# Window attention and a squared-ReLU layer pair on one core: batch 1 turned by DMA, batch 2 by seven products, 64-row sinks, an order table

## The chip, the core and the metric

The kernel runs on one core of one Trainium2 chip. The metric is device time in microseconds (us). A core has TensorE (PE, matmuls into PSUM), VectorE (DVE), ScalarE (ACT), GpSimd (POOL) and SyncE (SP), each with its own queue of instructions that it runs in program order, and 16 DMA engines. POOL's DMAs here are the ones that convert float32 to bfloat16 on the way (one queue, called q0 in the profile); SP's are plain DMAs and DMA transposes (q1).

## The reference

```python
# q, k, v: (4 batches, 8 heads, 768 positions, 64); n_sink 4, window 128
scores = (1/8) * q @ k^T
keep   = (key < 4) or (0 <= query - key < 128)
a      = softmax(where(keep, scores, -1e9))
x      = (a @ v), heads side by side          # (3072 rows, 512)
out    = max(x @ w_in, 0)**2 @ w_out          # w_in (512, 2048), w_out (2048, 512), float32 out
```

## The kernel before, in words

A batch has 768 rows, worked as three pairs of 128-row tiles (s, or u, = 0, 1, 2). Its stages:

- **Loads.** Batch 0's q and k for the first four tiles come by eight SP DMAs (L557) as float32 and are regrouped to bfloat16. Everything else comes through POOL: tiles of q, k or v (L578, L587, L606, L616; 256 KB read, 128 KB written) and four parts each of w_in (L514) and w_out (L522; 1 MB read, 512 KB written).
- **Turning q and k** so that head dimension lies on partitions. Batches 0 and 1: PE transposes (L708), then copies from PSUM by DVE or ACT. Batches 2 and 3 (`NATURAL`): one DMA transpose per tile on SP (L662), 12 per batch.
- **Attention** per pair of tiles and pair of head pairs (m): scores on PE with 64 rows of the array for each head (L815), exp on ACT (L836), masks on DVE or POOL, values on PE (L884), normalisation on DVE (L900, L901). The four sink keys of all heads are scored by L774 into `es`; for s of 1 and 2 each head's values take one more 128-row matmul `es` x `vs` in which all rows but that head's four are zero.
- **Turning the attention output** (bridge): PE transposes (L933) and copies in batches 0 and 1, DMA transposes on SP (L915) in batches 2 and 3.
- **Layer 1.** Classic (L965): four matmuls per block of 128 hidden units, ReLU on ACT or DVE, square on DVE or ACT. Fast (batch 3, `FAST`): seven products of half size instead of eight (L1085), in six quads; each quad needs sums of x (L1043), a copy and two subtractions of PSUM (L1126), a ReLU, and a final add with ReLU on DVE (L1153). Five sums of w_in (L1009) come first.
- **Layer 2.** Classic (L1174) for the first two pairs of batch 0, else seven products of half size (L1284) with sums of the squares (L1242) and of the results on DVE, then a store by SP.

Every step is an `op` with what it follows, the buffers that it takes and gives back, and the engines that may run it. `Plan.run` writes the program: it always picks the ready step with the earliest start by its own table of costs, changed by `SHIFTS`, a list of offsets for every step. POOL's loads are chained in one fixed order: v tiles 0 and 1, w_in 0, v tiles 2 and 3, the other w_in parts, batch 0's last k and q tiles and v tiles, w_out, then batch 1, 2 and 3.

A product of the fast layer 1 and its following wait, as an example of how steps are tied:

```python
m4 = product(4, 1, 3, False, [k2])      # k2: DVE has taken bank 1 out of PSUM
m3 = product(3, 0, 4, False, [k3])
k4 = op(..., relu, after=[m3, m4], takes=[r1s])
```

Of the kernel before, what the change touches and what calls it, by code (L numbers as in the profile page):

```python
# [12 lines left out]
FP32 = mybir.dt.float32  # L13
BF16 = mybir.dt.bfloat16
# [3 lines left out]
LATENCY = 0.135  # L18
PE_SLACK = 0.0
DMA_START = {"sp": 1.45, "act": 1.2, "pool": 1.6}  # L20
DMA_LATENCY = 0.9
WARM_UNTIL = 34.0
SHIFTS = {
# [9 lines left out]
    ('prep', 0, 0): ((-0.212, 1.23), (-0.072, -0.24), (-0.19, 0.16), (-0.726, 0.34), (0.102, 1.1), (-0.535, 0.02),  # L33
# [3 lines left out]
    ('sink', 0, 0): ((4.752, 1.43), (1.667, 2.03),),  # L37
    ('att', 0, 0): ((0.347, 0.31), (0.954, 0.9), (-0.499, -1.83), (0.762, -2.15), (0.932, -0.05), (-2.305, -7.94),
        (-0.09, 0.64), (-0.608, -0.19),),
    ('val', 0, 0): ((-0.669, 0.31), (-0.697, -0.27), (2.439, -2.91), (-0.554, 0.35), (-0.437, -0.15), (-0.471, 0.35),  # L40
        (-0.386, 0.35), (-0.377, 0.25),),
    ('turn', 0, 0): ((1.726, 0.79), (1.562, 0.69), (1.948, 1.13), (1.496, 0.73),),
    ('att', 0, 1): ((3.244, 0.46), (11.783, 1.08), (3.403, 0.48), (2.622, -0.1), (0.081, -0.49), (-0.044, -0.15),
        (11.287, 1.58), (1.317, -0.32), (2.357, -0.58), (1.537, 1.18), (-0.135, 0.19), (-0.111, -0.81),),
    ('val', 0, 1): ((-1.139, 2.3), (-0.295, 1.56), (-0.887, 1.68), (-0.625, 1.18), (-3.257, -5.22), (-3.374, -3.06),
        (-3.291, -3.92), (-2.551, -2.62),),
    ('turn', 0, 1): ((0.396, -1.51), (-0.815, -0.63), (-0.017, -0.23), (-0.694, 0.15), (-0.252, 1.39),),
    ('prep', 0, 1): ((0.244, -0.3), (0.839, 0.68), (-0.246, 0.32), (0.932, -0.62), (1.027, -0.56), (0.209, -0.32),),
    ('sink', 0, 1): ((1.975, -1.87), (0.782, -1.52),),
    ('att', 0, 2): ((0.244, -0.66), (-1.989, 0.29), (-0.493, 0.33), (0.159, -0.68), (1.032, 0.54), (0.796, 0.57),  # L50
        (-0.189, 0.02), (1.388, -0.12), (0.48, -0.01), (0.313, -0.14), (1.032, 0.72), (-1.933, -0.09),),
    ('val', 0, 2): ((-0.074, -1.39), (-0.782, 0.91), (-0.843, -3.97), (-0.333, 0.47),),
    ('turn', 0, 2): ((0.672, -0.31), (-0.118, -0.09), (0.809, -0.71), (2.596, 0.84),),
# [6 lines left out]
    ('prep', 1, 0): ((-3.284, 0.24), (-1.096, -0.94), (0.605, -0.58), (0.247, -2.12), (-5.483, 0.49), (0.694, 0.02),  # L60
        (0.597, -0.24), (0.597, -0.24), (-8.208, 1.17), (0.681, -1.4), (-1.5, -0.64), (0.357, -0.54), (-10.29, 0.97),
        (0.494, -0.72), (0.633, -0.24), (-0.776, -0.16), (0.529, -0.04), (-1.768, -0.84),),
    ('sink', 1, 0): ((0.868, 0.19), (0.763, 0.03),),
    ('att', 1, 0): ((-0.287, -0.2), (-4.964, -0.65), (-1.435, -0.81), (-3.607, -0.91), (-2.001, -0.01),
        (-0.447, -0.1), (-0.674, 0.1), (-0.719, -0.6), (-0.604, 0.18), (-0.781, -0.2),),
    ('val', 1, 0): ((-6.954, 1.31), (0.072, -4.26), (-0.107, -0.44), (-0.058, -0.46),),
    ('turn', 1, 0): ((-4.522, 0.82), (-0.734, 2.5), (-1.073, 0.44), (0.276, 0.05),),
    ('att', 1, 1): ((1.003, 0.22), (1.223, 0.6), (0.413, -0.45), (0.232, -0.07), (0.259, -0.21), (0.322, -0.07),
        (1.914, -1.56), (0.055, 0.01), (0.085, -2.03), (0.176, 0.47),),
    ('val', 1, 1): ((0.205, 0.29), (-0.249, -0.53), (-2.761, 0.71), (0.377, -0.27),),  # L70
    ('turn', 1, 1): ((0.754, 1.22), (2.068, -0.78), (0.857, 1.68), (-4.788, 1.81),),
    ('prep', 1, 1): ((2.397, 1.96), (5.859, 1.94), (-0.449, 1.75), (1.83, 1.58), (1.97, 1.7), (0.173, -0.21),),
    ('sink', 1, 1): ((0.987, -0.02), (-0.036, -5.62),),
    ('att', 1, 2): ((1.119, -4.28), (0.959, -0.36), (0.499, 1.02), (0.438, -0.34), (1.738, -0.38), (0.767, 0.25),
        (1.547, -0.3), (1.332, 0.31), (1.014, 0.54), (0.269, -2.08),),
    ('val', 1, 2): ((1.128, -0.41), (3.047, 0.37), (3.469, 0.88), (2.416, -3.47),),
    ('turn', 1, 2): ((-4.356, -7.65), (-0.607, -0.19), (-1.006, 0.46), (-4.587, -4.53),),
# [5 lines left out]
    ('sum', 0, 2): ((0.045, -1.68), (0.204, -1.02), (-0.718, -2.55), (0.064, -1.38),),  # L83
# [115 lines left out]
        (0.268, 1.28),),  # L199
    ('ev', 3, 2): ((1.463, 6.42), (-1.377, 1.64), (0.142, -5.03), (-0.286, -3.32), (-0.494, 0.4), (-0.624, -0.94),  # L200
        (-0.804, -0.94), (-1.227, -0.94), (-0.047, -3.46),),
}


class Slot:
# [16 lines left out]
class Plan:  # L222

# [1252 lines left out]
```

## Time and profile before

| | us |
|---|---|
| three runs | 216.72, 217.82, 218.05 (median 217.82) |
| span of the profiled execution | 216.0 |
| PE busy | 206.5 (96%) |
| DVE busy | 161.5 (75%) |
| ACT busy | 123.2 (57%) |
| POOL busy | 98.7 (46%) |
| read from HBM, written | 27.30 MB, 6.29 MB |

The span runs from the first to the last instruction of one execution; the runs are whole executions, so the median is compared with the span through their difference, 1.8 us. A busy PE counts the modelled length of each matmul, which overlaps with the next one's start; how fast matmuls really follow each other is read from the starts. The granted TensorE clock is 1.000. The table of stretches gives, for each stretch, busy us of PE, PE's weight loads, DVE, ACT, POOL with the number of instructions, then granted clock, DMA share and GB/s. In DMA views a queue's share counts the time of its packets, which overlap, so it can be over 100%; its megabytes are those written.

### The profile page before, as it was taken

To read this page: it belongs to the slowest core of one execution; us is meant where nothing else is said; L and a number is where in the kernel's file an instruction comes from. 1 tells how busy PE (TensorE), PEld (TensorE's weight loads), DVE (VectorE), ACT (ScalarE), POOL (GpSimd) and SP (SyncE) were. 2 spreads that over 40 slices of the span, in tenths; PEclk is the share of its full clock that TensorE was granted. 3 is DMA by queue.
4 is the path that set the end of the run, shared out by engine and by line. 5 is a ranking of instruction groups with operands and counts; after the bars stand their busy time and mean duration, and the time that the engine had idled before them with its cause. 6 is when DMAs were issued, how large, how long until landed. Compare 5 with 4: busy or idle time off the path is not lost.

```text
span 216.0 us, 5470 instructions
## 1 busy us (share of the span) xinstructions
PE 206.5 (96%) x2287; PEld 165.4 (77%) x2287; DVE 161.5 (75%) x292; ACT 123.2 (57%) x158; POOL 98.7 (46%) x137
## 2 busy tenths in 40 slices
PE   3999999999999999999999999999999998999993
PEld 3858996689486755688887965598898998897882
DVE  6487458773958569688689994477995859999973
ACT  2498567366663775976757268566623369482100
POOL 7799773698935974898954424002302000000000
PEclk9999999999999999999999999999999999999999
DMA  5999999999997699999999936000023260000133
GB/s 156 261 182 206 174 199 213 160 154 205 156 147 169 88 147 133 167 108 147 142 199 133 139 84 209 3 0 0 3 97 75 52 219 3 2 0 5 55 132 107
DMA packets 93625, 26.09 MB, mean 121 GB/s; under 512 B 86816, under 2 KB 91552, under 8 KB 93600
## 3 DMA queue, kind: packets, MB, share of 16 engines
q0 software_dynamic: 69248, 12.59, 80.3%
q1 hardware_dynamic: 24168, 13.07, 28.1%
q8 instruction: 18, 0.29, 0.6%
q10 hardware_dynamic: 184, 0.07, 0.1%
q14 instruction: 7, 0.06, 0.1%
HBM read 27.30 MB, written 6.29 MB: 156 GB/s over the span
## 4 chain that ended last, share of the span: by engine, by line
PE 73%; DVE 14%; ACT 3%; DMA 3%; issue 3%; SPq 2%; DVEq 0%; ACTq 0%
PE pm L965 29%; PE py L1284 20%; PE po L884 6%; PE py L1174 6%; PE ps L815 5%; PE pm L1085 4%; DMA qr<-in_q_dram 3%; DVE sg L1242 3%; ACT expm L836 2%; DVE t L1126 2%; DVE r L1153 2%; SPq L557 2%; PE px L933 1%; DVE gT_sb L1109 1%; DVE expm L848 1%
## 5 line engine op out<-in xcount | busy, mean ns | idle before, releaser
L965 PE MATMUL pm<-xT,w_in_sb 128*128 128x256 bf16 (+1 forms) x448 | 66.1, 304 | 0.0
L965 PEld LDWEIGHTS <-w_in_sb 128*128 128x128 bf16 x448 | 48.3, 114 | 13.4 <-issue 1.3
L836 ACT ACTIVATE expm<-ps 128x1024 bf16<-128x1024 f32 (+1 forms) x48 | 43.7, 951 | 18.1 <-PE ps L815 17.5
L426 POOL TENSOR_SCALAR_AFFINE_SELECT expm<-expm 128x512 bf16<-128x512 bf16 x36 | 27.3, 787 | 55.9 <-ACT expm L836 43.7
L976 ACT ACTIVATE r<-pm 128x1024 bf16<-128x1024 f32 x30 | 30.7, 1023 | 17.3 <-PE pm L965 15.6
L1284 PEld LDWEIGHTS <-gT_sb 128*128 128x128 bf16 x336 | 31.2, 98 | 4.3 <-issue 0.7
L987 DVE TENSOR_TENSOR gT_sb<-r 128x1024 bf16<-128x1024 bf16 x26 | 19.3, 741 | 17.3 <-ACT r L976 17.1
L1284 PEld LDWEIGHTS <-sg 128*128 128x128 bf16 x240 | 22.4, 98 | 4.5 <-DVE sg L1242 1.0
L1284 PE MATMUL py<-wt,sg 128*128 128x256 bf16 x160 | 20.8, 273 | 0.4 <-DVE sg L1242 0.4
L1284 PE MATMUL py<-wt,gT_sb 128*128 128x256 bf16 x160 | 20.8, 273 | 0.0
L1284 PE MATMUL py<-w_out_sb,gT_sb 128*128 128x256 bf16 x144 | 18.5, 273 | 0.0
L884 PEld LDWEIGHTS <-expm 128*128 128x128 bf16 x352 | 16.3, 97 | 2.5 <-issue 0.7
L901 DVE TENSOR_TENSOR xn_sb<-po,rc 128x512 bf16<-128x512 f32 (+1 forms) x28 | 17.2, 615 | 1.0
L884 PE MATMUL po<-v,expm 128*128 128x65 bf16 x352 | 17.5, 193 | 0.3 <-DVE xT L402 0.2
L1174 PE MATMUL py<-w_out_sb,gT_sb 128*128 128x512 bf16 x64 | 15.3, 380 | 0.0
L848 DVE TENSOR_TENSOR expm<-expm,tri 128x1024 bf16<-128x1024 bf16 x14 | 11.0, 791 | 5.1 <-ACT expm L836 4.9
L815 PE MATMUL ps<-qkT 64*128 64x256 bf16 (+1 forms) x256 | 14.6, 238 | 0.0
L815 PEld LDWEIGHTS <-qkT 64*128 64x128 bf16 x256 | 8.1, 94 | 7.1 <-issue 6.1
L884 PE MATMUL po<-vs,es 128*128 128x65 bf16 x128 | 12.9, 193 | 0.0
L400 ACT ACTIVATE osb<-py 128x256 f32<-128x256 f32 (+1 forms) x15 | 6.6, 441 | 10.2 <-PE py L1284 7.1
L884 PEld LDWEIGHTS <-es 128*128 128x128 bf16 x128 | 11.7, 97 | 0.0
L587 POOL DMA_DIRECT2D v<-in_v_dram x12 | 11.0, 927 | 0.2
(97 smaller groups left out, 330.5 us busy)
## 6 DMA issues: line engine op xcount, KB each, us to landing
out_dram<-osb SPq DMA_DIRECT2D x11, 512.0 KB, 3.7
v<-in_v_dram POOLq DMA_DIRECT2D x24, 128.0 KB, 7.5
qn<-in_k_dram POOLq DMA_DIRECT2D x20, 128.0 KB, 7.5
qn<-in_q_dram POOLq DMA_DIRECT2D x20, 128.0 KB, 7.4
w_in_sb<-in_moe_w_in_dram POOLq DMA_DIRECT2D x4, 512.0 KB, 10.3
w_out_sb<-in_moe_w_out_dram POOLq DMA_DIRECT2D x4, 512.0 KB, 10.2
qr<-in_k_dram SPq DMA_DIRECT2D x4, 256.0 KB, 5.7
qr<-in_q_dram SPq DMA_DIRECT2D x4, 256.0 KB, 5.3
```

Source lines behind the costliest of these rows:

```text
L426: nc.gpsimd.affine_select(out=e_tile, in_=e_tile, compare_op=ALU.is_ge, fill=fill, base=i - 1, pattern=[[0, n], [1 if i else -1, 128]], ch ...
L587: return [nc.gpsimd.dma_start(out=v_sb[b % 2][:, t, :, 0:D], in_=v[b, :, 128 * t:128 * t + 128, :].rearrange("h p d -> p h d"))]
L815: nc.tensor.matmul(ps[:, h2, o:o + w], lhsT=qkT_sb[r, m, 1, c, :], rhs=qkT_sb[r, m, 0, qb:qb + w // 128, :], start=(i == 0 and not biased) ...
L836: nc.scalar.activation(out=x[:, :, o:512], in_=bank_t["s", b, s, m][:, :, o:512], func=AF.Exp, scale=scale)
L848: nc.vector.tensor_mul(y, y, tri.rearrange("p (o a) c -> p o (a c)", o=1).to_broadcast([128, 4, 256]))
L884: touch(("po", b, s, m0), e, nc.tensor.matmul(pv[:, i, h2, :], lhsT=lhsT, rhs=rhs, start=(n_ == 0), stop=(n_ == len(mms) - 1)), j)
L901: touch(("po", b, s, m0), e, nc.vector.tensor_tensor(out=xn_sb[:, 2 * s:2 * s + 2, 128 * (m0 + j0):128 * (m0 + j0 + nj)].rearrange("p i (j ...
L965: nc.tensor.matmul(pm[:, i, :], lhsT=w_in_sb[:, fb // 4, kb, fb % 4:512:4], rhs=xT[:, c0 // 256:(c0 + cw) // 256, kb, :], start=(kb == 0), ...
L976: nc.scalar.activation(out=o, in_=h, func=AF.Relu)
L987: nc.vector.tensor_mul(g, r, r)
L1174: touch((b, u), e, nc.tensor.matmul(pm[:, i, :], lhsT=gT_sb[:, fb, 128 * t:128 * t + 128], rhs=w_out_sb[:, fb, :], start=(fb == 0), stop=( ...
L1284: ins = nc.tensor.matmul(y_, lhsT=x[:, i, :], rhs=r_, start=(first or tail and n == 2) and i == 0, stop=i == HB - 1, skip_group_check=not ...
```

## The change

Six things change together.

1. `NATURAL` becomes (1, 2, 3): batch 1's 12 q and k tiles and its six tiles of attention output are turned by DMA transposes on SP.
2. `FAST` becomes (2, 3): batch 2's layer 1 goes by seven products as well. The sums of w_in are made before batch 2; two of the five overwrite parts of w_in that are no longer read.
3. Sinks: a step of its own ahead of the values, two matmuls of 64 rows and 130 columns for each of two heads' pairs, each on its half of the array and into its own PSUM bank. For that, head pairs m and m + 2 go together where m and m + 1 did.
4. Buffers: PSUM is one pool of four double banks (was two of two), and the work tiles of `expm`, `r` and `sg` share 15 buffers; which buffer a step gets is fixed when the program is written.
5. POOL's loads are no longer chained among themselves.
6. `Plan.run` no longer chooses. The order of all 880 steps, each with its engine (p PE, v DVE, a ACT, g POOL, s SP) and a number of idle-filling matmuls (+n), stands in a table, `ORDER`.

```diff
+ORDER = """
+8s 55a 9s 10s 11s 12s 13s 0v 14s 1v 56v 15s 36g 27g 61v 7a 28g 32g 3g 57p 58p+4 59a 60v 63p+22 33g 31g 67a 6g 19g 5g
+65v 68v 83p 62a 64p+1 69p 73v 75p+8 71v 70p 20g 66a 85a 114p 91p 74a 29g 76p 30g 21g 22g 79g 4g 23g 77v 72v 116a 78v
+104p 93a 107a 92p+1 84p 80v 117v 24g 39g 86a 51g 115p 87p 89p+4 118a 94a 88v 90v 130p 133p+2 37g 135a 81p+1 95p 134v
...
+156p 158p 35g 46g 173a 159v 176a 163p 203s 178p 157a 193p 194a 179a 190p 169p 187p 191a 188a 168v 184p 181p 164v
+170a 165v 180v 185a 174a 47g 268p 189a 219p 43g 34g 264v 182v 269p 222a 186a 345g 44g 200s 363s 347g 352g 201s 54g
+270p 212p 353g 202s 41g 48g 205s 368s 369s 215a 213a 220a 271p 272p 49g 204s 228p 231a 273p 236p 229a 274p 171v 208v
+192v 209v 195v 265v 351g 367s 275p 42g 129g 221v 290v 214v 348g 361g 354g 239a 232v 266v 223v 366s 346g 364s 370s
+177v 237a 254p 279p 276v 280p 277v 360g 374s 358g 357g 586g 359g 372s 238g 588g 255a 257a 216v 246p 210p 371s 278s
...
+234p 242p 235v 350g 183a 296a 283p 284p 243v 245s 365s 226s 258g 250g 285p 300v 244s 293v 259p 260p 261v 298p 301p
+267v 395p 303v 287v 396a 286p 288a 227s 398a 302p 592g 305p 304v 306v 307v 248g 600g 595g 599g 613s 308s 604s 606s
+18s 356g 349g 362g 611s 593g 601g 386p 251p 252p 387a 389a 253v 421p 424a 330p 594g 422a 608s 397v 375v 388v 403p
+315p 598g 596g 589g 406a 407g 404a 390v 331v 391p 377p 316a 378a 262s 263s 587g 399v 405v 392v 318p 379p 319a 380a
+312p 382a 413p 416a 313v 314a 414a 317v 489v 383v 321p 408p 309p 355g 310a 322a 332a 417v 488v 490v 324p 591g 605s
+409p 327p 336p 325a 328a 311v 326v 320a 381v 384p 337a 410v 385v 425v 329a 323a 607s 338a 333p 289s 609s 615s 393s
...
 class Plan:
-    def run(self):
...
+    def run(self, order):
+        for word in order.split():
+            n, _, dummies = word.partition("+")
+            o, e = self.ops[int(n[:-1])], {"p": "pe", "v": "dve", "a": "act", "g": "pool", "s": "sp"}[n[-1]]
...
             o.run(e)
...
-    sizes = dict(att=2, den=2, qr=5, qs=6, expm=8, r=3, osb=2, sg=4, u=2)
+    sizes = dict(ps=4, qr=5, qs=6, w2=15, osb=2, u=2)
...
-    NATURAL, TURNED, BIASED, FAST = (2, 3), (), 1, (3,)
+    NATURAL, TURNED, BIASED, FAST = (1, 2, 3), (), 1, (2, 3)
+    CHAINED = False
...
+                    if s:
+                        def sinks(e, s=s, m0=m0, bo=bo):
+                            po = bank_t["o", b, s, m0] = tile_of(bo, "po", [128, 2, 512], FP32)
+                            for i in range(2):
+                                for j in range(2):
+                                    r, m, c = slice(64 * j, 64 * j + 64), m0 + 2 * j, 128 * (2 * s + i - 2)
+                                    touch(("po", b, s, m0), e, nc.tensor.matmul(
+                                        po[:, j, 2 * (D + 1) * i:2 * (D + 1) * (i + 1)].rearrange("p (h d) -> p h d", h=2),
+                                        lhsT=es[r, c:c + 128], rhs=vs[r, 2 * m:2 * m + 2, :],
+                                        start=(i == 0), stop=False), j)
...
-                                        if t >= 2:
-                                            mms.append((i, h2, es[:, 128 * (t - 2):128 * (t - 2) + 128], vs[:, h, :]))
...
-                nc.vector.tensor_tensor(out=wi_sb[name], in0=x, in1=y, op=how)
+                if n >= 3:
+                    wi_sb[name] = [x[:, 0], x[:, 1]]
+                    nc.vector.tensor_tensor(out=x, in0=x, in1=y, op=how)
+                    return
```

The steps of the table that the prediction speaks of. On POOL: 36g and 33g load w_out parts 3 and 0, 34g part 1; 27g and 28g batch 0's k tiles 4 and 5, 29g and 30g its q tiles 4 and 5; 32g, 31g, 19g, 20g its v tiles 5, 4, 0, 1; 21g loads w_in part 0; 37g to 54g are batch 1's 18 tiles, 345g to 362g batch 2's, 586g to 603g batch 3's (355g is v tile 2 of batch 2). On SP: 196s to 207s turn batch 1's tiles (204s the k tile 4), 226s, 227s, 244s, 245s, 262s, 263s its output, 278s and 308s are stores. On PE: 87p is the first values step of batch 0, 160p its first layer 1 step, 254p the first scores of batch 1's third pair, 409p the first values of batch 2's second pair; 120p, 144p, 109p, 153p, 241p, 233p and so on are sink steps.

More of the change, by code (lines that the diff above doesn't have):

```diff
@@ L299, in run @@
+    def run(self, order):
+        free = {p: list(range(n)) for p, n in self.capacity.items()}
+        emitted = set()
+        for word in order.split():
+            n, _, dummies = word.partition("+")
+            o, e = self.ops[int(n[:-1])], {"p": "pe", "v": "dve", "a": "act", "g": "pool", "s": "sp"}[n[-1]]
+            assert e in o.engines and all(id(a) in emitted for a in o.after + o.follow)
             for s in o.takes:
-                free[s.pool].sort()
-                free[s.pool].pop(0)
@@ L302, in run @@
-            self.now, self.gap = start, start - engine.get(e, 0.0)
+                s.buf = free[s.pool].pop(0)
+            self.dummies = int(dummies or 0)
             o.run(e)
-            engine[e] = start + cost
-            end = start + cost
-            if o.dma:
-                moved = [y.end - DMA_LATENCY for y in o.yields]
-                queue[e] = max([queue.get(e, 0.0), end + DMA_START[e]] + moved) + o.dma
-                end = queue[e] + DMA_LATENCY + o.margin
-                landed.setdefault(e, []).append(end)
@@ L311, in run @@
-            o.engine = e
-            o.end, o.issued = end, start + cost
+            emitted.add(id(o))
             for s in o.reads:
                 s.readers -= 1
-                s.end = max(s.end, end)
                 if not s.readers:
-                    free[s.pool].append(s.end)
-            for u in users.get(id(o), ()):
-                blockers[id(u)] -= 1
-                if not blockers[id(u)]:
-                    ready.append(u)
-        return max(o.end for o in self.ops)
+                    free[s.pool].append(s.buf)
@@ L992, with weight_sums_in @@
     wi_sb, wi_slot = {}, {}
-    def weight_sums_in(key, after):
+    def weight_sums_in(first):
         P.group = ("wi", 0)
         A = [[w_in_sb[:, 2 * i:2 * i + 2, 2 * j:2 * j + 2, :] for j in range(2)] for i in range(2)]
-        spare = qkT_all[0].rearrange("p (n i a f) -> n p i a f", n=3, i=2, a=2)
+        after = [o for x, o in ops.items() if x[0] == "layer1" and x[1] < first] + list(w_in_op.values())
+        spent = [ops[x] for x in ops if x[0] in ("scores", "sinks") and x[1] == 2]
+        slots = [Slot("qr", 99), Slot("qr", 99)] if first == 1 else None
+        tiles = {}
         for n, (name, x, y, how) in enumerate(((1, A[0][0], A[1][1], ALU.add), (2, A[1][0], A[1][1], ALU.add),
@@ L1119, in first @@
         def first(e):
-            T["t"] = work["expm"].tile([128, nb, hw], FP32, name="t", tag="expm")
+            T["t"] = tile_of(ts, "t", [128, nb, hw], FP32)
             touch(tag, e, copy(e, T["t"], T["y"][:, 0]), 0)
-        k1 = op(key(1), {"act": 0.6, "dve": 0.64}, first, after=[m1], takes=[ts])
+        k1 = op("first", "act dve", first, after=[m1], takes=[ts])
         def less(bk):
@@ L1404 @@
     for b in range(B):
         if b == 0:
-            at = attention(0, lambda f: f - 1.0)
-            at(0, 0.0, 1.0, ("den", "att"))
-            late["masks"] = op(0.006, {"pool": 1.0}, build_masks, after=[c_tri, ops["bridge", 0, 0]])
-            at(1, 0.2, 0.725, "att")
-        if b == 0:
+            at = attention(0)
+            at(0)
+            late["masks"] = op("masks", "pool", build_masks, after=[c_tri])
+            for g in range(1, len(GROUPS[0])):
+                at(g)
             for i in range(4):
@@ L1436 @@
[L1436 to L1442 removed]
+            at = attention(b + 1)
+            for g in range(len(GROUPS[b + 1])):
+                at(g)
+        if b == 0:
+            weight_sums([w_out_op[i] for i in range(4)])
```

824 lines of the change are left out of this document (316 added, 508 removed), and 72 rows, old and new, of the table SHIFTS.

## The prediction

> **What bounds the kernel now.** First the page: span, busy shares, the chain that ended last.
>
> ```profile
> span 216.0 us, 5470 instructions
> PE 206.5 (96%) x2287; PEld 165.4 (77%) x2287; DVE 161.5 (75%) x292; ACT 123.2 (57%) x158; POOL 98.7 (46%) x137
> ...
> DMA  5999999999997699999999936000023260000133
> ...
> PE 73%; DVE 14%; ACT 3%; DMA 3%; issue 3%; SPq 2%; DVEq 0%; ACTq 0%
> ```
>
> PE is busy 96%, but the DMA row shows nines in nearly all of its first 23 slices of 5.4 us (to 124 us): a second resource is full in the same time. Second, the stretches table:
>
> ```profile
> 0.00:17.30 17.30, 13.58 (x177) 10.30 (x178) 11.80 (x33) 9.92 (x13) 14.44 (x30) 1.00 1.18 200
> 17.30:170.00 152.70, 152.15 (x1685) 117.85 (x1684) 112.67 (x197) 94.57 (x119) 84.28 (x108) 1.00 1.35 129
> 170.00:200.00 30.00, 28.41 (x303) 26.19 (x302) 26.53 (x42) 17.30 (x23) 0.00 (x0) 1.00 0.14 46
> ```
>
> From 17.3 to 170 us PE (second figure) waits for 0.55 us in all, so every load now lands in time. From 170 to 200 us, batch 3's fast layer 1, it waits 1.6 us with DVE at 88%. Third, the DMA view of three stretches: 30 to 38 us (weights alone), 40 to 48 (128 KB tiles almost alone), 61 to 67 (tiles and turns):
>
> ```profile
> q0 software_dynamic: 461, 1.69, 105.5%
> ...
> q0 software_dynamic: 9591, 1.21, 252.4%
> ...
> q0 software_dynamic: 3228, 0.41, 133.5%
> q1 hardware_dynamic: 2176, 0.52, 68.2%
> ```
>
> A w_out part (0.524 MB) takes 8/1.69 x 0.524 = 2.5 us, and a tile (0.131 MB) 8/1.21 x 0.131 = 0.87 us. In 61 to 67 us, POOL's queue q0 moved 0.41 MB, which alone takes 2.7 us; that leaves 3.3 us for q1's 0.52 MB, four turns, **0.8 us per turn**. The two queues share one resource; they do not add. [...]
>
> **The change, part by part, on PE.**
> - Batch 1's turning leaves PE: 48 transposes (32 and 16) and 24 bridge transposes, 8 of which take 0.45 us (50.04 to 50.49): 72 x 0.056 = 4.0 us off. Their 18 evacuations leave DVE and ACT.
> - Batch 2's layer 1: classic, 64 matmuls of 512 columns at 0.216 (16 in 3.5 us) and 64 of 256 at 0.109 (16 in 1.75) make 20.8 us. Fast, 112 of 128 columns at 0.056 and 112 of 256 at 0.109 make 18.5. 2.3 us off on PE. In wall time batch 3's fast layer 1 ran from 172.10 to 193.16, 21.1 us, because DVE could not follow; so the gain is bounded by 0 and 2.3. I take 2.3 here, as batch 2's products are laid between other PE work, and pay DVE below.
> - Sinks: 128 matmuls of 128x65 at 0.031 (48 in 1.45 us) = 3.9 us become 64 of 64 rows and 130 columns. The trace has 64-row pairs in the scores: a pair runs together. Two pairs of 130 columns are 0.11 us, 16 steps 1.8 us. But a visit to 64-row matmuls costs extra:
>
> ```profile
> 74.51 3.64 PE L965 MATMUL pm<-xT,w_in_sb 128*128 128x512 bf16 x16
> ...
> 78.09 0.62 PE L815 MATMUL ps<-qkT 64*128 64x128 bf16 x12
> ...
> 78.64 1.70 PE L965 MATMUL pm<-xT,w_in_sb 128*128 128x512 bf16 x7
> ```
>
> 16 x 0.216 = 3.46 us, yet the scores start after 3.58: 0.12 on the way in. Twelve score matmuls hold PE 0.55 us, six 0.33 (32.58 to 32.91), so 0.12 is fixed, on the way out. Of the 16 sink steps in the table 8 stand next to scores or to each other; the rest make 12 more changes of shape, 1.4 us. Net 0.7 off (2.1 without these waits). [...]
> - Sum on PE: 4.0 + 2.3 + 0.7 = **7.0 us off**.
>
> **On DVE**: 12 more subtractions at 0.68, 6 final steps at 1.22, 2.9 us of sums are 18.4; 9 copies at 0.42 come from ACT, 12 squares at 0.74 and 2 relus at 1.22 go to it, and the turned tiles' evacuations go. Net about +11, to 172 us.
>
> **On the DMA engines and queues**: the bytes loaded stay; 18 turns come, 18 x 0.8 = 14.4 us, all in the part that is full. They also stand in SP's queue, where a turn issues in 1.25 us and holds what is behind it (other turns, stores). And the order changes. POOL's queue now begins with w_out part 3, batch 0's k tiles 4 and 5 and v tile 5, w_out part 0, v tile 4, and only then v tiles 0 and 1; w_in part 0 is the eleventh load, where it was the third. Batches 2 and 3 are loaded ahead of tiles that batch 1 and 2 still lack. Each engine runs its own steps strictly in the table's order, so a PE step whose tile has not landed holds all PE work behind it.
>
> **What is late next, by sums.** Three gates.
> - First values (87p): needs v tiles 0 and 1. Ahead of them on the DMA engines: 8 q/k loads (2.1 MB, 8.4 us, as 1.55 MB moved in the six from 2 to 8 us), two w_out parts 5.0, six tiles 5.2; from 2.3 us this gives 21. Now PE starts values at 13.24. PE has about 1.3 us more work ahead of it than now, so some 6 us are lost.
> - Scores of batch 1, third pair of tiles (254p): needs turn 204s. Now the engines are full to 67.0 us with all weights, q/k, 37 tiles, 4 turns and a store (check: 2.3 + 8.4 + 20 + 32.4 + 3.2 + 1.3 = 67.6). The table asks for the same weights and q/k, 30 tiles and 15 turns: 67.0 - 6.1 + 8.8 - 1.3 = 68.4, plus 2.5 from issue to landing of the last turn (what a turn of xT takes): **70.9**. PE's own work to there is 43 us plus 3.5 of shape changes from 6.3 us: it could be there at 53.
> - Values of batch 2 (409p): needs v tile 2 of batch 2, placed behind 13 tiles of batch 3. From 67.0: 22 tiles 19.3, 29 turns (four of them of batch 1's output) at 0.75, one store 1.3: 109. PE from 254p arrives at 70.9 + 33.7 + 24 x 0.12 = 107.5. So **109**.
> Behind 409p, PE has by the same prices 110.0 us of streaming (61 + 2 layer-2 products at 0.875, 84 quarter products at 0.44, classic layer 1 8.7, the rest attention) and 22 changes of shape, 2.6. From the last matmul to the end are 3.6 now (212.4 to 216.0): 225.2. By its rows DVE has about 110 us left there for PE's 112.6, a higher share than the 88% at which PE lost 1.6 us of waits and 3 of wall in 170 to 200; for two fast batches I add 3 (bounds 0 and 7): span 228. The runs' median stands 1.8 above the profiled span (217.82 against 216.0): **229.5 us**.
>
> The bounds of the unknowns: a turn by itself moved 0.23 MB/us in the best microseconds, 0.55 us, which takes 4 us off the gates; a fully shared stretch with idle queues between (SP and POOL each wait in order) adds 5. A long PE wait is covered by nothing: PE's queue holds no other work.
>
> **The rivals.**
> - *The loads are hidden* (faster): PE gets all it needs, because the DMA engines take SP's turns and early q/k beside POOL's loads at no cost. It decides at 204s: POOL's queue alone would be through there at 1.6 + 8 x 2.5 + 30 x 0.87 = 48 us, before PE's 53. For it: the table fits that pace closely, and PE waits for no load now. Against it: 61 to 67 us. Time: 217.8 - 7.0 + 2 for DVE = 212.8; with free shape changes and the full fast gain 209.
> - *Cheap turns* (slower, less): turns at 0.55 and few waits: 254p at 66, 409p by PE at 102.6: 102.6 + 112.6 + 3.6 + 2 + 1.8 = 222.6.
> - *The change does not do what it says on PE*: sinks save nothing, the fast layer 1 takes the 21.1 us that batch 3's takes: 7.0 becomes 4.0; with hidden loads 214 to 216.
> - *DVE becomes the bound*: 7 instead of 3, and gates 4 later: 237.
>
> **How the numbers follow.** The gated case 0.66 (224 to 238), cheap turns 0.12 (219 to 224), hidden loads 0.15 (208 to 215), PE parts without gain 0.07, about 216 with loads hidden for the most part. The forecast is 229.5. The range 216 to 238 leaves out hidden loads and a little above. One per cent, 2.2 us, is about what a measurement of this kernel tells from no change. Faster 0.16, same 0.06, slower 0.78.
>
> **What would show it.** PE idle before the first values until about 21 us and before the third scores of batch 1 until about 70, both with a DMA as releaser; the DMA row without its dip at slices 12 and 13; 72 transposes fewer; DVE near 172. Wrong would be: PE busy through 17 to 70 us, or scores of batch 1 with their turns landed by 55.

## The result, and the profile after

The changed kernel takes **245.38 us** (median of four runs, 243.74 to 248.19) beside 217.94 for the kernel before: a ratio of 1.125, 95% interval 1.120 to 1.129. It is slower, as forecast, but by 27.4 us where 11.7 were forecast, and 7 us above the top of the range. The profiled execution took 243.83 us. Ratios leave out runs more than 1.5% above the fastest of their kernel (here the fourth, 248.19), medians do not, so where the two differ the ratio counts.

From its page: the span, busy shares, PE's granted clock, the DMA engines and the chain that ended last.

```profile
span 242.1 us, 5377 instructions
PE 206.4 (85%) x2219; PEld 165.2 (68%) x2224; DVE 164.8 (68%) x312; ACT 123.1 (51%) x151; POOL 97.5 (40%) x132
...
PEclk9959999998597799958999999999999999999998
DMA  6999999999999999999999233335003320040104
...
PE 51%; DMA 32%; DVE 8%; POOL 3%; SPq 2%; issue 2%; ACT 1%; POOLq 0%; DVEq 0%; ACTq 0%
```

The dip of the DMA row at slices 12 and 13 is gone, DMA holds 32% of the chain (3% before), and PE is at half its clock in several slices, which it never was before. The table of stretches, cut at the gates of the prediction (first values 21.41 us, end of the wait of batch 1's third scores about 80.2, values of batch 2 about 124, last matmul 238.2):

```profile
0.00:21.41 21.41, 11.86 (x110) 8.29 (x111) 8.38 (x21) 8.82 (x12) 15.57 (x30) 0.84 1.34 193
21.41:55.00 33.59, 30.95 (x383) 28.32 (x384) 16.39 (x40) 19.14 (x24) 21.11 (x28) 1.00 1.82 166
55.00:80.20 25.20, 12.67 (x75) 5.04 (x76) 14.72 (x24) 9.19 (x11) 13.94 (x19) 0.79 1.88 140
80.20:124.00 43.80, 38.38 (x358) 21.95 (x362) 23.62 (x44) 21.95 (x26) 30.73 (x42) 0.89 1.91 157
124.00:238.20 114.20, 112.50 (x1301) 101.64 (x1299) 101.67 (x186) 63.76 (x81) 16.15 (x17) 1.00 0.33 68
```

The kernel before, over the two stretches in the middle:

```profile
55.00:80.20 25.20, 24.96 (x279) 16.39 (x277) 17.93 (x37) 15.23 (x22) 17.65 (x25) 1.00 1.62 141
80.20:124.00 43.80, 43.56 (x517) 34.31 (x516) 36.70 (x60) 28.83 (x35) 30.18 (x38) 1.00 1.96 146
```

From 55 to 80.2 us PE executed 75 matmuls where the kernel before executed 279. A second way to see it is PE's work still to be done at a given time: the sum over the matmuls that start later, each by its shape at the rates of the prediction, idle-filling ones left out.

| PE work left, us, at | 0 | 21.4 | 55 | 80 | 124 |
|---|---|---|---|---|---|
| before | 190.3 | 180.5 | 147.6 | 124.7 | 83.3 |
| changed | 182.0 | 177.6 | 149.8 | 141.9 | 110.1 |

The change takes 8.3 us of work from PE. They are used up by 30 us; some 15 us are lost from 55 to 80 and 10 more from 80 to 124; after that nothing. PE's waits in the changed kernel (waiting line, releaser; total us, times, longest):

```profile
PE ps L529 <- DMA qkT<-qn: 14.9, 4, 6.4
PE pt L425 <- POOL ident L224: 5.1, 1, 5.1
PE pt L425 <- DVE qs L181: 4.1, 1, 4.1
PE pm L685 <- DMA xT<-xn_sb: 2.2, 1, 2.2
```

L529 are scores, `qkT<-qn` a DMA transpose of a q or k tile: four waits on turned tiles (before 219p at 62.34, 228p at 72.00, 254p at 80.13, 386p at 102.66), and one on batch 1's turned output (330p at 107.13). The chain that leads to 254p (start, length, what):

```profile
30.52 14.52 DMA qn<-in_k_dram
45.94 14.17 DMA qn<-in_k_dram
60.40 12.76 DMA qn<-in_k_dram
73.18 6.91 DMA qkT<-qn
80.13 0.93 PE ps L529 x10
```

Three tiles, each 13 to 14.5 us from issue to landing (7 to 8 in the kernel before), follow one another because POOL issues each only when the eighth before it has landed (at 45.94 and 60.40 us, behind landings at 45.04 and 60.11); then SP turns the last of them in 6.9 us.

### The profile page after: what moved, and what is told of

It reads as the page before. It is cut to its first block, busy times and chain, and to the rows that moved or that the text cites. A ratio compares the mean times of both kernels' runs of the same rounds, so it can differ in the third digit from the quotient of the medians.

```text
span 242.1 us, 5377 instructions
## 1 busy us (share of the span) xinstructions
PE 206.4 (85%) x2219; PEld 165.2 (68%) x2224; DVE 164.8 (68%) x312; ACT 123.1 (51%) x151; POOL 97.5 (40%) x132
## 4 chain that ended last, share of the span: by engine, by line
PE 51%; DMA 32%; DVE 8%; POOL 3%; SPq 2%; issue 2%; ACT 1%; POOLq 0%; DVEq 0%; ACTq 0%
PE py L1024 20%; DMA qn<-in_k_dram 17%; PE pm L825 13%; PE pm L685 10%; DMA qn<-in_q_dram 5%; DMA xT<-xn_sb 4%; DMA qr<-in_k_dram 3%; DMA qkT<-qn 3%; PE po L608 3%; DVE r L893 2%; PE py L914 2%; PE ps L529 2%; POOL qn L328 1%; DVE sg L982 1%; SPq L639 1%
## 5 line engine op out<-in xcount | busy, mean ns | idle before, releaser
L549 ACT ACTIVATE expm<-ps 128x1024 bf16<-128x1024 f32 (+1 forms) x48 | 43.8, 952 | 38.6 <-PE ps L529 38.5
L685 PE MATMUL pm<-xT,w_in_sb 128*128 128x256 bf16 (+1 forms) x320 | 45.9, 301 | 3.1 <-DMA xT<-xn_sb 2.2
L685 PEld LDWEIGHTS <-w_in_sb 128*128 128x128 bf16 x320 | 34.5, 115 | 11.1 <-issue 4.9
L529 PE MATMUL ps<-qkT 64*128 64x128 bf16 (+1 forms) x256 | 16.8, 260 | 15.3 <-DMA qkT<-qn 14.9
L529 PEld LDWEIGHTS <-qkT 64*128 64x128 bf16 x256 | 9.1, 101 | 24.6 <-issue 17.2
L339 POOL DMA_DIRECT2D v<-in_v_dram x24 | 21.4, 895 | 9.5 <-DVE rc L623 3.6
L825 PE MATMUL pm<-xs,w_in_sb 128*128 128x128 bf16 (+1 forms) x256 | 24.6, 246 | 0.0
L328 POOL DMA_DIRECT2D qn<-in_k_dram x20 | 17.7, 888 | 14.9 <-DMA qn<-in_k_dram 10.1
L825 PEld LDWEIGHTS <-w_in_sb 128*128 128x128 bf16 x256 | 22.0, 114 | 0.6 <-issue 0.4
L328 POOL DMA_DIRECT2D qn<-in_q_dram x20 | 17.8, 894 | 4.7 <-DMA qn<-in_k_dram 2.1
L914 PE MATMUL py<-w_out_sb,gT_sb 128*128 128x512 bf16 x59 | 17.9, 451 | 0.4 <-issue 0.3
L847 ACT ACTIVATE gT_sb<-r 128x1024 bf16<-128x1024 bf16 x17 | 17.4, 1051 | 0.7 <-DVE r L893 0.5
L825 PEld LDWEIGHTS <-qkT 128*128 128x128 bf16 x192 | 16.3, 114 | 0.3 <-issue 0.2
## 6 DMA issues: line engine op xcount, KB each, us to landing
qn<-in_k_dram POOLq DMA_DIRECT2D x20, 128.0 KB, 11.7
qn<-in_q_dram POOLq DMA_DIRECT2D x20, 128.0 KB, 11.7
```

Of the source, the lines that this page charges most:

```text
L328: nc.gpsimd.dma_start(out=qn_t[b, ti][:, t, :].rearrange("p (h d) -> p h d", d=D), in_=(q, k)[ti][b, :, 128 * t:128 * t + 128, :].rearrang ...
L339: nc.gpsimd.dma_start(out=v_sb[b % 2][:, t, :, 0:D], in_=v[b, :, 128 * t:128 * t + 128, :].rearrange("h p d -> p h d"))
L529: nc.tensor.matmul(ps[:, h2, o:o + w], lhsT=qkT_sb[r, m, 1, c, :], rhs=qkT_sb[r, m, 0, qb:qb + w // 128, :], start=(i == 0 and not biased) ...
L549: nc.scalar.activation(out=x[:, :, o:512], in_=bank_t["s", b, s, m][:, :, o:512], func=AF.Exp, scale=scale)
L685: nc.tensor.matmul(pm[:, i, :], lhsT=w_in_sb[:, fb // 4, kb, fb % 4:512:4], rhs=xT[:, c0 // 256:(c0 + cw) // 256, kb, :], start=(kb == 0), ...
L825: touch(tag, e, nc.tensor.matmul(y[:, bk, i, :], lhsT=weights(name, f0 + i, a), rhs=rhs[:, a, :], start=fresh and i == 0 and a == 0, stop= ...
```

## The experiments

Theory A: the loss is batch 1's turns, which share the DMA engines with the loads. Theory C: it is the half clock behind PE's waits. Theory B: it is the order of POOL's loads. Later two more were needed: O, the table asks for late tiles in any case, and W, turns beside weight loads slow the DMA engines. "The replay" in the expectations is a model that runs the table's steps in order, at prices from the trace. "+x" is against the kernel before in the same comparison.

**e1: copies for turns.** Batch 1's 18 tiles are copied by SP, not turned, so that part of the computation is left out.

```diff
+  if b == 1:
+      nc.sync.dma_start(out=qkT_sb[:, :, ti, t, :], in_=qn_t[b, ti][:, t, :]...)
+      return
   nc.sync.dma_start_transpose(...)          # the same for xT
```

> The changed kernel with its order table, but each of batch 1's 18 DMA transposes is a plain DMA copy of the same 128 KB between the same tiles (left out: the turning itself, so batch 1's numbers have no meaning). Theory A, the turns fill the DMA engines (in the changed kernel's trace a turn among loads has about 1.05 us of them): replaying the steps in the table's order with prices from the trace gives 226 us of span if a copy costs nothing and 232 if its 512 packets go at the 1195 packets per us of POOL's tiles, so a time of 228 to 234. Theory B, the order in which POOL's loads stand makes the loss: the loads stand as before, so 240 to 244. Theory C, the half clock after each wait: it goes as far as the waits go, between the two.

Measured 230.34 us, ratio 1.059 (1.055 to 1.063): 15 us of the 27 go. The third scores run at 70.2 us, the values of batch 2 at 109.6. Issue to landing of what SP moved from 33 to 57 us, first in e1, then in the changed kernel (KB, then median us):

```profile
qkT<-qn SPq DMA_DIRECT2D x9, 128.0 KB, 7.1
```

```profile
qkT<-qn SPq DMA_TRANSPOSE x8, 10.4
```

Packets say more. In e1, from 33 to 57 us, a copy's 1024 B packets took 59 ns on average, tiles' 32, w_in's 98 and w_out's 324; the last three are what they take in the kernel before with no copy beside them, so no load's packets took longer beside the copies. In the changed kernel, from 40 to 42.5 us, where two turns stood beside w_in part 3, tiles' packets took 55 to 151 ns on average and turns' 83 to 110 (31 beside tiles alone), and the three kinds together came to 626 packets of tiles, 283 of turns and 30 of w_in in 2.5 us, which alone take 1.1. So it is not the bytes that cost. But a copy is 128 packets of 1024 B, not the 512 that the expectation assumed, and a turn is 512 of 256 B: whether the transposing costs or the number of packets, no run tells apart.

**e2: idle-filling matmuls in the waits**, so that the clock stays up.

```diff
-63p+22 219p    228p    254p    386p
+63p+90 219p+105 228p+55 254p+42 386p+48
```

> The changed kernel with idle-filling matmuls ahead of five steps that wait (63p 90 instead of 22, 219p 105, 228p 55, 254p 42, 386p 48), so that TensorE is not idle there and its granted clock should stay at 1.0. Theory C (the half clock after waits is a large part of the unforeseen 16 us): 232 to 238. Theory A: the work after a wait is done sooner but the next turn lands no sooner; the replay without any half clock is 1.6 us shorter, so 241 to 244.

Measured 246.57 us, ratio 1.133 (1.128 to 1.138). That is above both expectations. Granted clock 0.986 instead of 0.94, and nothing gained: the five waits end at 63.2, 75.5, 83.2, 106.6 and 111.2 us, none earlier than the changed kernel's 62.3, 72.0, 80.1, 102.7 and 107.1, because DMAs end them. Theory C fell as the cause of the loss; as the turns also landed later here, the run doesn't tell what the clock alone is worth.

**e3, e4: orders from a search.** All six parts, or all but batch 1's turns (`NATURAL` (2, 3)), with a table found by searching on a replay of the trace (costs from its rows, a turn among loads at 1.05 us).

```diff
-ORDER = """ 8s 55a 9s 10s 11s 12s 13s 0v 14s ...
+ORDER = """ 8s 0v 27g 34g 29g 30g 28g 3g 9s ...      (e3)
+ORDER = """ 8s 9s 10s 55a 7a 67a 0v 1v 27g ...       (e4, NATURAL = (2, 3))
```

> All six parts of the change, the same 880 steps, but in another order, searched with prices from the changed kernel's trace (a turn among loads 1.05 us, queues sharing packet by packet). Theory A: the turns stay, so no order gets below the kernel before; the replay says 224 of span, 226 us. Theory B: with a good order the parts gain what they take off PE, 209 to 214.

> The change without its first part: batch 1 is turned by PE and PSUM copies as in the kernel before; seven products in batch 2, 64-row sinks, shared buffers and an order table (searched with the same prices as the one before it) stay. Theory A: the replay says 213.4 of span, 215 us, faster than the kernel before and 11 less than the whole change in its new order. Theory B: the part undone is not the cause, so within 3 us of the whole change in its new order.

Both missed. e3 took 262.02 us (ratio 1.204, 1.198 to 1.210): its turns stand beside weight parts from 42 to 86 us. e4 took 228.37 us (1.050, 1.045 to 1.055): weights were placed so late (the last packet at 70 us) that batch 2's turns stood beside them, and one took from 46.8 to 57.3 us. The replay's price of a turn did not hold there.

**e5, e6: the head.** In the changed kernel's table v tiles 0 and 1 go ahead, the two early w_out parts behind; e6 with e1's copies as well (batch 1 not turned).

```diff
-36g 27g 28g 32g 33g 31g 19g 20g 29g 30g 21g 22g 23g
+27g 28g 19g 20g 32g 31g 29g 30g 21g 22g 23g 36g 33g      (POOL's loads; all else stays)
```

> The changed kernel, its order table with one edit at the head of POOL's queue: v tiles 0 and 1 trade places with v tiles 5 and 4, and the two early parts of w_out (36g, 33g) stand behind v tile 3. Everything else as in the table. Theory B (each gate costs for itself): the first values come at about 17 instead of 21.4 us and the 4 us are kept, 238 to 240. Theory A (the DMA engines, loaded with turns, set when batch 1's scores can run): the first values come as early, but the 4 us are lost again before the third scores of batch 1 (still at about 78 to 81 us), 243 to 246; the replay says 241 to 242 of span.

> Both edits: the head of POOL's queue in the new order, and batch 1's 18 turns as plain copies (the turning is left out). Theory A: with the turns cheap the gain at the head is kept, some 4 us less than the copies alone (230.3): 224 to 228. If the head's gain is lost here too (within 1.5 us of 230), something else than the turns sets the pace.

e5: 246.3 us, ratio 1.131 (1.127 to 1.134). First values at 17.84 instead of 21.41, and all of it lost by 40 us, as w_in lands later. e6: 232.09 us (1.065, 1.060 to 1.070), no better than e1, above the 224 to 228 of theory A and also outside the 1.5 us about 230 that would have pointed elsewhere. With the DMA engines full, the loads moved ahead delayed others (in e5 PE waits 3.2 us for w_in, 0.9 in the changed kernel); theory B fell in this form.

**e7, e8: the search again**, with a turn among loads dearer: e7 without batch 1's turns, e8 with all parts.

```diff
+ORDER = """ 8s 0v 27g 3g 29g 9s 2v 10s 11s ...       (e7, NATURAL = (2, 3))
+ORDER = """ 8s 0v 9s 1v 10s 11s 19g 12s 13s ...      (e8)
```

> The change without its first part again (batch 1 turned by PE), in an order searched with costlier prices for DMA: a turn beside weight parts three times as long, turns and tiles landing later than the trace's median, so that the order leaves slack where the first search left none. Theory A: the replay with those prices says 219.7 of span; with the prices of the traces less: 214 to 221. Theory B: no better than the whole change in an order searched in the same way.

> The whole change in an order searched with the same costlier prices. Theory A: batch 1's turns keep it above the kernel before and some 10 to 15 us above the same search without them: 228 to 238. Theory B: 214 to 222, as without the part.

e7 took 227.87 us (1.043, 1.038 to 1.048), e8 258.9 and 272.1 in its two runs, both kernels above everything expected. e7's PE works nearly without a gap from 37 us on, but has 157.8 us of work left at 55 (147.6 before): these tables lose their time in the head. So they could not price the parts, and a better start was needed.

**e9 to e11: parts priced from the order of the kernel before.** Each step gets the place of its counterpart in the profiled execution of the kernel before, and the search only improves on that, with dear DMAs.

```diff
-NATURAL, TURNED, BIASED, FAST = (1, 2, 3), (), 1, (2, 3)
+NATURAL, TURNED, BIASED, FAST = (2, 3), (), 1, (2, 3)      (e9; ORDER = 8s 0v 55a 7a 9s 2v ...)
+NATURAL, TURNED, BIASED, FAST = (2, 3), (), 1, (3,)        (e10; ORDER = 8s 0v 9s 55a 5g 6g ...)
+NATURAL, TURNED, BIASED, FAST = (1, 2, 3), (), 1, (3,)     (e11; ORDER = 8s 9s 10s 67a 56a 55a ...)
```

> Batch 1 turned by PE as before, batch 2 by seven products, 64-row sinks, shared buffers; the table now starts from the order that the kernel before ran in (each step at the place of its counterpart, sinks steps just ahead of their values, batch 2's products where batch 3's stood, 46 us earlier), improved by a search in which every DMA is dear. Order theory (what e4 and e7 lost against before, 10 us, came from the searched tables, in the first 55 us): 212 to 218 us, PE's work remaining at 55 us about 147 to 149, no wait of PE above 1.5 us behind 20 us. Parts theory (the 64-row sinks, the shared buffers or batch 2's products cost it by themselves): 222 or more, with the loss in the stretch of that part (for batch 2's products 125 to 160 us).

> Only the 64-row sinks and the shared buffers with a fixed table; batch 1 turned by PE, batch 2's layer 1 classic, the table made as in e9 from the order of the kernel before. By the prediction's terms the sinks save 0.7 us on PE: order theory 214 to 219; parts theory 222 or more. The difference between this and e9 is batch 2's seven products: the prediction's gain of 2.3 us on PE, bounds 0 and 2.3.

> Batch 1's 18 turns by DMA with the 64-row sinks and shared buffers, batch 2's layer 1 classic; the table made as in e9 from the order of the kernel before, the turns a few us behind their loads. If the turns cost what e1 showed in the changed kernel's table (15 us, in which PE's 4 us saved are lost as well): 226 to 235, with PE's waits on turned tiles of batch 1 between 45 and 95 us. If their loss was an accident of the two tables: 214 to 221. Above 240: turns are dearer still when they stand beside parts of weights, as in e3 and e8.

e9: **214.61 us**, ratio 0.987 (0.981 to 0.992), faster than both kernels. e10: 217.48, ratio 1.0005 (0.998 to 1.003). e11: 223.64, ratio 1.025 (1.018 to 1.032). Each has a table of its own, and only one, so a price here is that of a part with its table. So read, sinks and buffers are worth nothing that can be told from none, batch 2's products 217.48 - 214.61 = 2.9 us of gain, and batch 1's turns 223.64 - 217.48 = 6.2 us of loss by the medians, 5.3 by the ratios; e11's time lies between its two expectations. From e9's page:

```profile
span 212.7 us, 5517 instructions
PE 203.0 (95%) x2298; PEld 166.6 (78%) x2303; DVE 174.6 (82%) x309; ACT 126.5 (59%) x164; POOL 102.6 (48%) x142
...
DMA  5999999999999999999978995600023223100205
```

Its DMA row is as full as the changed kernel's to 100 us, and PE works 95% of the span: a full DMA row alone says nothing on the time.

**e12: the whole change, that kind of table**, and nothing else changed.

```diff
-ORDER = """ 8s 55a 9s 10s 11s 12s 13s 0v 14s ...
+ORDER = """ 8s 0v 9s 10s 67a 55a 11s 12s 61a ...
```

> The changed kernel with nothing but its table replaced by one made as in e9 and e11 from the order of the kernel before. If the parts add up in comparable tables (e10 +0.0, batch 2's products 214.6 - 217.5 = -2.9, batch 1's turns 223.6 - 217.5 = +6.2): 219 to 224 us, and then some 22 of the 27 us that the change lost are its table's. If the whole needs more of the DMA engines than any order can hide, as e3 and e8 suggested: 235 or more.

Measured 228.16 us, ratio 1.046 (1.040 to 1.052): between the two. The parts add up to 220.8 (219.9 by the ratios) and the whole is 7 to 8 us above that, but some 17 of the 27 us are the table's. The same two stretches in e12:

```profile
55.00:80.20 25.20, 23.56 (x259) 17.51 (x257) 21.39 (x35) 13.14 (x17) 12.47 (x16) 1.00 1.31 145
80.20:124.00 43.80, 39.61 (x381) 28.42 (x380) 25.16 (x44) 30.45 (x37) 19.49 (x25) 1.00 1.68 141
```

The third scores of batch 1 run at 78.67 (246p) and 80.25 us (254p) here, no earlier than in the changed kernel, but without a wait. The table has put 14 us more of other work ahead of them: at 80 us 127.6 us are left, not 141.9. All of batch 1's 12 q and k turns are issued between 48.4 and 64.4 us, behind the last weight part, and landed by 69.6; the changed kernel's run from 32.1 to 80.1.

**e13: the weights first.** Four loads of the changed kernel's table are moved. **e14: turns early.** In e12's table batch 1's 12 turns are moved up, each behind its load.

```diff
-24g 39g 51g 37g 50g 25g 45g 26g 38g 52g 40g 35g 46g 47g 43g 34g
+24g 25g 26g 35g 34g 39g 51g 37g 50g 45g 38g 52g 40g 46g 47g 43g        (e13, POOL's loads)
-37g 36g 39g 50g 34g 46g 43g 53g 44g 45g 32g 35g 40g ... 199s 201s 202s 203s ...
+37g 196s 36g 39g 198s 50g 205s 34g 46g 203s 43g 200s 53g 44g 201s 45g 202s 32g 35g 40g 199s ...   (e14)
```

> The changed kernel's table with four POOL loads moved: w_in parts 2 and 3 and w_out parts 2 and 1 right behind w_in part 1, so that the weights are through by about 42 us, before batch 1's turns; nothing else moves. Theory W (turns that stand beside weight parts slow the DMA engines; that is what made the changed kernel's DMA 5 us late by 55 us): the wait of the third scores of batch 1 ends 4 us earlier, at about 76, and the time is 236 to 242. Theory O (the table's loss is that PE's steps ask for late tiles in any case): 244 to 248.

> The kernel of e12 with batch 1's 12 turns moved up in SP's queue, each right behind its tile's load in the table, so that they stand from about 33 to 60 us, beside w_out parts 3, 1 and 2, where e12 has them from 48 us on, behind the last weight part; everything else stays. If a turn costs the same wherever it stands, its tiles are turned up to 15 us earlier and the time is 226 to 229, e12's, or less. Theory W: the weight parts land later, layer 2 of batch 0 waits for w_out at about 50 us by some 5 us or more, and the time is 232 to 240.

e13: 240.77 us, ratio 1.107 (1.103 to 1.110), 4.6 us below the changed kernel; 254p's wait ends at 77.2, 2.9 earlier (4 were expected). Its waits on turned tiles, 14.9 us in the changed kernel, are:

```profile
PE ps L528 <- DMA qkT<-qn: 10.9, 3, 4.7
```

e14: 239.01 us, 1.101 (1.096 to 1.106), 10.9 us above e12, with turns that are only issued earlier (and in another order among themselves; PE's waits on turned tiles are only 1.0 us). e14's waits:

```profile
PE py L913 <- DMA w_out_sb<-in_moe_w_out_dram: 3.8, 1, 3.8
PE po L607 <- DMA v<-in_v_dram: 3.7, 1, 3.7
```

Layer 2 of batch 0 waits for w_out, then values for a v tile. Issue to landing, from 33 to 57 us, in e14 and then in e12:

```profile
w_out_sb<-in_moe_w_out_dram POOLq DMA_DIRECT2D x1, 512.0 KB, 14.7
...
qkT<-qn SPq DMA_TRANSPOSE x8, 9.2
```

```profile
w_out_sb<-in_moe_w_out_dram POOLq DMA_DIRECT2D x1, 512.0 KB, 9.7
qkT<-qn SPq DMA_TRANSPOSE x6, 5.8
```

Theory W's forecasts, 236 to 242 and 232 to 240, held in both directions. That weights are the only thing that turns must not stand beside doesn't follow; the table below shows that they aren't.

**e15, e16: second tables** for the whole and for the change without batch 1's turns, from the same start with other random numbers.

```diff
+ORDER = """ 8s 55a 0v 9s 10s 67a 1v 11s 56v ...      (e15)
+ORDER = """ 8s 55a 0v 9s 1v 3g 5g 19g 20g ...        (e16, NATURAL = (2, 3))
```

> The whole change with a second table, from the same start and search as e12's, other random numbers. If e12's 228.2 is what the parts cost in a table of that kind: 225 to 232. If it was luck, good or bad: outside of 222 to 235, and the split of the loss into parts and table stays open by as much.

> The change without batch 1's DMA turns, as e9, with a second table from the same start, searched on. If e9's 214.6 stands for the parts and not for its table: 212 to 216, faster than the kernel before. Luck of e9's table: 217 or more.

e15: 234.84 us, 1.077 (1.072 to 1.083), above the 225 to 232 expected and inside the 222 to 235 beyond which the split would stay open; e16: 214.98 us, 0.987 (0.983 to 0.991). Without the turns the time hardly hangs on the table, with them by 7 us. e15 again has turns beside weights: its first goes at 30 us, its last weight packet at 62.

What the DMA engines did from 20 to 60 us, at fixed prices: a tile is 1024 packets at 1206 per us, a w_in part 512 at 190, a w_out part 128 at 50.5, each from a stretch in which its kind ran alone, and a turn 512 at 660, as beside tiles from 65 to 67 us of the kernel before. With nothing beside them turns reach 970 packets per us (118 to 119 us); at 930 the rows with turns fall by 0.1 to 1.6 us and keep their order, but for e14 and e4. Stores are left out (the kernel before has one, 1.3 us).

| kernel | turns ahead of the last weight packet | work done in 40 us |
|---|---|---|
| before | 0.2 | 38.4 |
| e9 | 0 | 39.9 |
| e12 | 0.1 | 39.3 |
| e13 | 0 | 38.7 |
| e14 | 3.7 | 37.3 |
| e4 | 4.2 | 37.2 |
| e7 | 0.2 | 37.2 |
| e11 | 5.1 | 36.9 |
| changed | 3.9 | 35.0 |
| e3 | 11.1 | 34.3 |
| e15 | 4.1 | 33.4 |

In the six kernels of this table that have several turns beside weight parts, 3 to 7 us of the engines' 40 are lost; in the others at most 1.6, but for e7, which loses 2.8 (1.3 us of work in the four from 28 to 32 us, with w_in packets of up to 964 ns and no turn near). The loss isn't in proportion to the number of turns (3 us in e11 with 5.1, 7 in e15 with 4.1), so no price per turn follows.

Turns beside tiles alone lose time too. Counted by single microseconds from 20 to 100 us at the same prices, the changed kernel loses 3.6 us in the 15 that have turns and weights and 4.5 in the 44 that have turns and tiles only; e12 loses 4.4 us in 35 with tiles only; e4 only 0.8 in 12 with weights. So weights more than double the loss per microsecond in the changed kernel (0.24 us against 0.10), but they aren't its only cause. One rival no run here tests: in the 18 traces, from 20 to 200 us, 105 packets of 16 KB on the instruction queue (q8) came while turns ran, and 89 of them were followed within 2.2 us by at least five packets of over 400 ns; without turns it was 5 of 158, and at moments with turns but no instruction packet near, one in five. About half of all such stalls (83 of 161) begin behind an instruction packet, so this too is not the whole of it.

## Why the prediction was right or wrong

- **Direction and mechanism: right.** Full DMA engines, a table that runs strictly in order, and turns and tiles that come late.
- **First gate: right in its number, partly by luck.** 21 forecast, 21.41 measured. The v tiles did land then (21.37 and 22.44), but PE itself got to 87p only at 21.10: it had waited 4.1 us at 12.70 for the regrouped q and k of batch 0, whose SP loads landed late, and ran at half clock from 11.5 to 18.3. So the forecast sign, PE idle until 21 us with a DMA as releaser, shows as only 1.1 us of wait. "Some 6 us are lost" fits: 5.4 by 21.4 us, and all 8.3 that PE saves by 30.
- **PE's parts: right in sum.** 7.0 us off forecast. By the work table 8.3 come off, less 18 changes of shape (12 were forecast) at 0.12 us, 2.1: 6.2. Sinks 0.7 forecast; e10 shows 0.1 slower, with an interval from 0.4 faster to 0.7 slower and its table's part in it: no more can be said. Batch 2's products 2.3 forecast, 2.9 measured (e9 against e10).
- **DVE: too dear.** 164.8 us busy, not 172: the sum of +11 adds 18.4 + 3.8 - 8.9 - 2.4 and leaves out the evacuations that it says go. 3 us of waits were added for two fast batches; from 409p to the last matmul the changed kernel takes 114.2 us where 112.6 was the sum without them, so 1.6 came, and e9 gains the whole saving with DVE busy 82%. The rival that DVE binds is out.
- **Second gate: the step that failed.** "0.8 us per turn" plus "2.5 from issue to landing" gave 70.9; measured 80.1. The price came from a stretch where turns had only tiles beside them. The table places 3.9 turns beside weight parts, and 5 us of the engines' 40 were lost. The 2.5 came from the wrong row of the page before, that of the attention output, turned from 94.5 us on; the turns of q and k had a row of their own, which stood above it (issues, median us to landing):

```profile
qkT<-qn SPq DMA_TRANSPOSE x24, 6.7
xT<-xn_sb SPq DMA_TRANSPOSE x12, 2.5
```

The last turn took 6.9 us, behind two turns of batch 2. Of the 9.2 us that the gate is late, 4.4 are this turn's landing; the other 4.8 are its tile, the 38th load, which landed at 73.2 where the sum has 68.4 (e12's 38th lands at 62.0). e13 takes the weights out of the turns' way and the gate moves 2.9 us, so the cause is shown for that part; for the rest of the tile's delay it stays open.
- **Third gate: 109 forecast, 123.9 measured.** 9.2 of the 14.9 are inherited. The step "PE from 254p arrives at 70.9 + 33.7 + 24 x 0.12" took PE to run without waits. It waited 2.8 us at 386p for a turn of batch 2 and 2.2 at 330p for batch 1's turned output, and ran at half clock from 103.7 to 110.5; its arrival, not the v tile (landed at 122.8), set the gate. The tile's own sum failed as well: it landed 14 us after the 109 forecast, and its 29 turns were priced at 0.75 where the second gate has 0.8.
- **Behind it: right** within 1 us (118.1 to the end against 119.2).
- **"A fully shared stretch with idle queues between adds 5"**, the upper bound of the turns, was too small and with it the range: 9.2 and 5.7 us at the two gates, against 5.
- **What the sums could not say**: a late gate costs what the table has behind it. e12 runs the same scores at the same 80 us, without a wait, and is 17 us faster. The prediction priced the gates of this table and so was bound to it; it took the loss for a price of the parts. By the runs the parts cost 10 to 17 us in the two tables made from the old order (e12, e15), all of it batch 1's turns (e9 and e16 without them are 3 us faster than before), and the changed kernel's own table another 10 to 17. Of these e13 gets 4.6 back with four loads. The other part, e13 against e12, is no matter of DMA throughput (38.7 and 39.3 in the table above); that it is the placing of PE's steps is argued from the work left at 80 us (138.9 and 127.6), not shown by a run of its own.
- **Half clock: not foreseen.** Filling the waits gained nothing, as DMAs end them (e2). Behind the last one, where no wait on a DMA follows at once, it did cost: eight L685 matmuls from 107.13 took 3.53 us, where eight of that shape took 1.85 at full clock (from 82.72 us in the kernel before). No run isolates this 1.7.
- **Two slips that move no gate**: 2.1 MB at 1.55 MB in six us are 8.1 us, not 8.4, and 228 + 1.8 is 229.8, not 229.5.
- The rivals *hidden loads* (PE's 14.9 us of waits), *cheap turns* (1.125) and *PE parts without gain* (e9) are out.

## What to carry to other kernels

A turn's price read beside one kind of load did not hold here beside another (its packets took 31 ns beside tiles alone, 83 to 110 with w_in there as well, in the changed kernel): read the transposes' price beside each kind of load that they will meet, and issue them behind the large loads, even if they then start 15 us later (e12 against e14, 228.16 and 239.01 us). Price a change in more than one order before calling the loss its own; here five of the six parts together gain 3 us (e9, e16), and the sixth, batch 1's turns, costs 5 to 20 us depending on the order that it stands in (e11 against e10, e15 against e16). And when a wait moves, ask what work the order has left behind it, not only when it ends.

## What the runs showed of the hardware

**Transposes beside other DMAs.** In e14, from 38.5 to 40.5 us, turns ran beside the tail of w_out: 244 tile and 263 turn packets in 2 us, which alone take 0.6; single packets took up to 1980 ns instead of 31. In e1 copies of the same bytes beside the same weights left all packets at their own times (59 ns, tiles' 32, w_in's 98, w_out's 324). Beside tiles, with no stall, a turn is 512 packets of 256 B at 31 ns, 15.9 us of one engine's time, and e1's copy 128 of 1024 B at 59, 7.6; with nothing beside them they take 20 and 46 ns, 10 and 5.9 us. So a turn took 2.1 times the engine time of a copy beside tiles and 1.7 times with nothing beside it, and far more in the stalls, beside weights above all. Stalls come beside tiles too: in the changed kernel packets took up to 1322 ns from 58.5 to 59.8 us, after the last weight packet at 55.6, and in the kernel before up to 1064 from 81.3 to 82.4. Why the packets stall isn't shown: the trace doesn't say which engine took a packet, and no run separates weights, tiles and the instruction packets.

**The clock.** In the changed kernel's trace each stretch of one granted clock but the last lasts 3.41 us or a multiple of it (3.41, 6.83, 20.48, 40.96, 129.71). Some of these windows (us, PE busy; the clock stands third from the end):

```profile
8.08:11.49 3.41, 0.49 (x8) 0.32 (x6) 0.00 (x0) 0.63 (x1) 2.85 (x6) 1.00 1.34 266
11.49:14.91 3.42, 2.21 (x16) 1.29 (x17) 2.50 (x5) 0.63 (x1) 1.27 (x2) 0.50 1.70 241
14.91:18.32 3.41, 3.41 (x30) 2.35 (x27) 2.14 (x4) 2.39 (x4) 1.82 (x3) 0.50 1.46 191
18.32:21.73 3.41, 3.02 (x36) 1.41 (x36) 1.71 (x4) 2.98 (x5) 3.15 (x8) 1.00 2.36 157
...
72.93:76.34 3.41, 3.05 (x19) 1.27 (x18) 2.62 (x4) 2.84 (x4) 1.75 (x2) 0.50 1.88 155
76.34:79.76 3.42, 1.37 (x8) 0.45 (x6) 3.14 (x5) 0.77 (x1) 2.51 (x4) 1.00 2.07 156
79.76:83.17 3.41, 3.04 (x16) 1.30 (x17) 1.82 (x4) 1.94 (x2) 3.11 (x5) 0.50 2.02 156
```

The clock of a window went here with PE's work in the one before, and at half clock it took more of it for a full one to follow. At full clock, 0.49 us of work (14%) and 1.37 (40%) were followed by half. At half clock, 2.21 us (65%) were followed by half again, 3.41 and 3.05 by full. Over the windows of all 18 traces whose clock is on record: at full clock, every one less than 44% busy was followed by half and every one over 55% by full; at half clock, none under 77% was followed by full and none over 85% by half.

**The queues.** Where tiles and turns both waited, their packets went about one for one, though a tile's have 128 B and a turn's 256 (in the changed kernel 411 and 415 from 78 to 79 us, 409 and 410 from 102 to 103, 410 and 409 from 108 to 109), so that the tiles got half of the bytes that the turns got. POOL had at most eight loads outstanding: in all 18 traces a load is issued only after the eighth before it has landed, by 0.28 us or more, so one slow weight part delayed the issue of the tiles behind it.
